# First product of the first layer by Strassen's scheme on two of three token chunks, and another order of blocks in the second layer

## The chip, the cores and the metric

The kernel runs on one core of a Trainium2 chip. The metric is device time in microseconds. Five engines work side by side: TensorE (PE) multiplies, VectorE (DVE) and ScalarE (ACT) do elementwise work and move results out of the matmul banks, GpSimd (POOL) and SyncE (SP) mostly issue DMA transfers. There are eight banks of 128 x 512 float32 into which PE accumulates.

## What is computed

Retention attention over 2 x 8 heads, 768 positions and 64 dimensions gives 1536 tokens of width 512. Two layers follow, each 512 to 2048 to 512; the weights arrive as float64.

```
state = gamma * state + k[t] (outer) v[t];  y[t] = scale * q[t] @ state
x = y as (1536, 512)
h = x @ w1_in;  g = max(h, 0) + log1p(exp(-|h|));  x = g @ w1_out
h = x @ w2_in;  g = h * clip(h + 3, 0, 6) / 6;     out = g @ w2_out
```

## The kernel before

**Number format.** Float64 weights are fetched as pairs of 32-bit words into `raw` tiles and put together into float32 (`cv` tiles) by ACT and DVE (class `Words`). Each float32 operand is split into a high and a low part, and a product is three matmuls: high by high, high by low, low by high. A weight tile `w` of 128 x 2 x 512 holds both parts.

**First layer.** Tokens come in three chunks of 512, the hidden width in 16 blocks f of 128. `gemm1` (G1) makes h for one chunk and one f: 4 slices of the contraction by 3 matmuls are 12 matmuls of 128 x 512. ACT copies h out, softplus runs on ACT and DVE (`e`, `g`, then `hi` and `lo`), and `gemm2` (G2), again 12 matmuls, adds the block into four banks (`acc`). On PE the order is G1 of unit s, then G2 of unit s - 2. All 32 weight tiles of this layer are made during chunk 0 and stay in 32 tiles of the on-chip memory for chunks 1 and 2.

**Attention.** Twelve units of 128 tokens (`attend`). Units 0 to 3 come first, 4 to 7 lie between the matmuls of chunk 0, 8 to 11 between those of chunk 1 (`spread(range(FIRST, NU), 2 * NF, 2.0)`, line 259, whose place is counted in G1 and G2). Units 8 to 11 fetch k and q also in turned blocks, by 32 small transfers each, 20 of them on SP and 12 on POOL.

**Second layer.** Tokens come in two blocks of 768, A and B. The first product is by Strassen's scheme: for a pair p of hidden blocks, seven products P1 to P7 of 6 matmuls of 128 x 384 take the place of eight. Their token operands are seven forms `xf` (sums and differences of quarters of x, made by `operands`), their weight operands four forms `wi` (made by `late_in`). A `step` is one block and one pair; its second product is 12 units of 3 matmuls of 128 x 512 into six banks (`out`), placed between the products of the next step. `STEPS` (line 243) runs A with p = 0 to 7, then B with p = 7 to 0. The forms `wi` of p < 4 go to memory and come back for B (`KEEP`), the weights of the second product come back for every step (`back`).

**What sets the order.** The list `pe` gives each task a due time; `Plan.run` then takes tasks by due time, the engines' free times, and the tiles that are free, and writes one fixed program for each engine. Every engine works through its program in order: an SP transfer that waits holds back those behind it.

Of the kernel before, what the change touches and what calls it, by code (L numbers as in the profile page):

```python
# [24 lines left out]
class Plan:  # L25


    LAG = {"PE": 0.30, "DVE": 0.12, "ACT": 0.16, "POOL": 0.16, "SP": 0.0}
    NEAR = {"PE": 0.5, "DVE": 0.15, "ACT": 0.15, "POOL": 0.3, "SP": 0.0}
# [17 lines left out]
    def __init__(self, tc):  # L47
        self.tc, self.tasks, self.pools, self.users, self.slot, self.groups = tc, [], {}, {}, {}, {}
        self.tensor, self.vector, self.scalar, self.gpsimd, self.sync = (
            self.Engine(self, getattr(tc.nc, e)) for e in ("tensor", "vector", "scalar", "gpsimd", "sync"))  # L50
# [22 lines left out]
    def run(self, log=None):  # L73
# [3 lines left out]
        left = {k: len(v) for k, v in self.users.items()}  # L77
        for _ in self.tasks:
            best = None
            for e, ts in todo.items():  # L80
                found = []
                for t in ts[:80]:
# [3 lines left out]
                    for pool in {p for p, _ in t.take}:  # L86
                        ok = self.places(pool, [k for p, k in t.take if p == pool])
                        if ok is None:
                            break
                        at = max([at] + [self.pools[pool][i] for i in ok])  # L90
# [11 lines left out]
            for pool in {p for p, _ in t.take}:  # L102
                keys = [k for p, k in t.take if p == pool]
                for key, i in zip(keys, self.places(pool, keys, at)):
                    self.pools[pool][i] = None
                    self.slot[key] = pool, i
# [27 lines left out]
def kernel(ctx, tc, q, k, v, w1_in, w1_out, w2_in, w2_out, table, out):  # L134
# [17 lines left out]
    KEEP = 4  # L152
    ONCE = 12
# [5 lines left out]
    EDGE = 9.0  # L159

    def BY_DVE(n):
        return n < 10 or n < 2 * NF and n % 4 != 0

# [13 lines left out]
    def x_of(part, c):  # L177
        key = part, c
        if key not in x_tiles:
            x_tiles[key] = (late_p if c == NC - 1 else fixed).tile([P, KD, CH], F32R, name=f"x_{part}{c}")  # L180
# [21 lines left out]
    def bank_groups(keys):  # L202
        kind, u = keys[0][0], keys[0][-1]
        if kind in ("h", "prod"):
            return [[0], [1]]
        if kind == "out":
            return [[2 + u]]
        if kind == "acc":
            return [[4, 5, 6, 7]]
# [4 lines left out]
    conv = [[("conv", m, i) for i in range(10)] for m in range(2)]  # L214
# [9 lines left out]
    room("w0", ONCE, [P, 2, CH], F32R)  # L224
    room("w", 2 * NF - LATE - ONCE, [P, 2, CH], F32R, later=[("arena", j) for j in range(LATE)])
    room("e", 2, [P, CH], F32)
    room("g", 2, [P, CH], F32)
    room("hi", 3, [P, CH], F32R)
    room("lo", 3, [P, CH], F32R)
    for name, n, shape, dtype in (("sums", 1, [P, 4, CH // 2], F32), ("xf", 7, [P, 2, 2, QT], F32R), ("tf0", 2, [P, 2, QT], F32), ("tf1", 2, [P, 2, QT], F32),  # L230
# [15 lines left out]
    cost.update(dict.fromkeys(PRODUCTS, PRODUCT))  # L246
    pe = [("Tk", 0), ("Tq", 0)]
# [11 lines left out]
    spread(range(FIRST, NU), 2 * NF, 2.0)  # L259
    n = 0  # L260
    for s in range(len(G)):
        for key in [("G1", s)] + ([("G2", s - LAG)] if s >= LAG else []):
# [3 lines left out]
    behind = [("G2", len(G) - LAG + i) for i in range(LAG)]  # L266
    for i in range(len(STEPS)):
        for name, n in PRODUCTS.items():
            pe += [(name, i)] + behind[:n]
# [23 lines left out]
    class Words:  # L293
# [47 lines left out]
        def made(self, at, fetch_at, load, give):  # L341
            T["F", self.key] = t0 = nc.add("SP", 0.45, self.fetch, due=fetch_at, take=[(f"raw{self.m}", self.raw_k)], load=load)
            t1 = nc.add("ACT", 0.65, self.bits, [t0], at - 3.5, take=[(f"cv{self.m}", self.cv_k)])
            if self.m:
# [9 lines left out]
    def weight(o, f, number):  # L354
# [3 lines left out]
        made = conv[0]  # L358
# [13 lines left out]
        part = [("w0" if number < ONCE else "w", ("w", key))]  # L372
        tail = 1.5 if BY_DVE(number) else 7.0
        t5 = x.made(use - tail, begin + 15 if number < 1 else use - tail - 8.0, 1.45 if o else 1.75, [x.raw_k])
# [7 lines left out]
        T["W", key] = [a, b]  # L382

    stash = ctx.enter_context(tc.tile_pool(name="stash", bufs=1, space=bass.MemoryType.DRAM))

    def kept(name):
        return stash.tile([P, 2 * CH], F32, name=name)

    def late_out(f):
# [4 lines left out]
        at = due["P1", f // 2] - 40.0 + 2.0 * f  # L394
        t = x.made(at, at - 10.0, 1.45, [])
# [4 lines left out]
        a = nc.add("ACT", ACS, lambda: nc.scalar.activation(part(0), x.w().bitcast(F32), AF.Copy), [t], at)  # L400
        b = nc.add("DVE", TT, lambda: nc.vector.tensor_tensor(part(1), x.w().bitcast(F32), part(0).bitcast(F32), ALU.subtract), [a], at + 0.7, give=[x.cv_k])
# [6 lines left out]
    def back(key, home, after, when):  # L408
        T["W", key] = [nc.add("SP", 0.45, lambda: nc.sync.dma_start(out=at_slot(key).rearrange("p a n -> p (a n)").bitcast(F32), in_=home),
                              [after], when, take=[("w", key)], load=1.6, hold=HOLD + when - 10.0)]  # L410

    def late_in(p):
# [3 lines left out]
        at = due["P1", p] - (20.0 if p else 12.0)  # L416
        t = [v.made(at + 2 * f, at - 10.0 + f, 1.75, [v.raw_k]) for f, v in enumerate(x)]
        sums = ("sums", ("sums", p))
        halves = slice(0, CH // 2), slice(CH // 2, CH)

        def word(f, j):
            return x[f].w().bitcast(F32)[:, halves[j]]

        def total(n):
            return at_slot(("sums", p))[:, n]
# [8 lines left out]
        s4 = nc.add("DVE", d, put(3, lambda: word(0, 1), lambda: total(1), ALU.subtract), [s2], at + 3.3)  # L434

        def pair(n):
            return at_slot(("sums", p))[:, n:n + 2].rearrange("p a n -> p (a n)")

        whole = slice(0, CH)
        for n, (source, cols, after, give) in enumerate((  # L440
                (lambda: x[0].w().bitcast(F32), whole, t, [x[0].cv_k]),
                (lambda: x[1].w().bitcast(F32)[:, halves[1]], halves[1], t, [x[1].cv_k]),
                (lambda: pair(0), whole, [s1, s2], [sums[1]]),
                (lambda: pair(2), whole, [s3, s4], [sums[1]]))):
            key = "wi", 0, p, n
# [577 lines left out]
```

## Time and profile before

| | us |
|---|---|
| median of 3 runs (576.94 to 577.71) | 577.46 |
| the profiled execution, its own time | 576.77 |
| its span, first to last instruction | 575.0 |
| PE busy | 565.5 |
| DVE busy | 386.9 |
| ACT busy | 334.9 |
| DMA traffic, MB | 91.08 |

The profile is of one execution. Busy is time in which an engine executes; matmuls overlap and their ends are modelled, so the distance between the starts of matmuls says more of PE than its busy time. A timeline row merges neighbours of one kind: start, length, engine, operation, tiles, shape, count, and in brackets the idle time before it and what ended it.

### The profile page before, as it was taken

How to read it: one execution, taken by the hardware profiler on the slowest of the kernel's cores; microseconds unless marked ns; L12 is line 12 of the kernel's file. 1: busy time of each engine (PE TensorE's matmuls, PEld its weight loads, DVE VectorE, ACT ScalarE, POOL GpSimd, SP SyncE). 2: the span in 40 equal slices, each digit the busy share in tenths (PEclk: the TensorE clock that was granted, in tenths of full speed). 3: DMA queues.
4: the chain of work that ended last, by engine and by line, in shares of the span. 5: the costliest groups of instructions: out<-in, count | busy, mean ns of one | idle time of the engine just before them, and what ended most of it. 6: DMA issues, size and time to landing. Idle time of an engine off the chain costs nothing.

```text
span 575.0 us, 9555 instructions
## 1 busy us (share of the span) xinstructions
PE 565.5 (98%) x3703; PEld 482.9 (84%) x3703; DVE 386.9 (67%) x694; ACT 334.9 (58%) x544; POOL 32.8 (6%) x61
## 2 busy tenths in 40 slices
PE   8999999999999999999999999999999999999996
PEld 7778788888788888888888988889988999888995
DVE  4999999994655446734889597997976544444342
ACT  3589889884333267945889596887644322222222
POOL 0000001044540000000000000000000000000000
PEclk9999999999999999999999999999999999999999
DMA  9998766613441206421655878486223595550003
GB/s 201 242 269 225 196 190 186 201 26 69 83 81 41 85 25 219 148 73 59 236 182 175 338 249 277 168 272 240 111 74 111 189 357 192 207 197 28 1 1 109
DMA packets 82157, 91.08 MB, mean 158 GB/s; under 512 B 48320, under 2 KB 65728, under 8 KB 82112
## 3 DMA queue, kind: packets, MB, share of 16 engines
q1 hardware_dynamic: 79856, 88.37, 48.6%
q0 software_dynamic: 2256, 2.10, 2.0%
q8 instruction: 29, 0.48, 0.3%
q14 instruction: 16, 0.13, 0.1%
HBM read 69.22 MB, written 19.92 MB: 155 GB/s over the span
## 4 chain that ended last, share of the span: by engine, by line
PE 94%; DVE 3%; ACT 2%; issue 0%; POOL 0%; ACTq 0%; DVEq 0%; POOLq 0%
PE banks L44 94%; DVE c L44 1%; ACT cv L44 1%; DVE raw L44 0%; ACT e L44 0%; ACT w L44 0%; DVE xf L44 0%; DVE cv L44 0%; ACT xf L44 0%; ACT parts L44 0%; ACT raw L44 0%; DVE parts L44 0%; DVE st L44 0%; ACT base L44 0%; DVE qT L44 0%
## 5 line engine op out<-in xcount | busy, mean ns | idle before, releaser
L44 PE MATMUL banks<-w,parts 128*128 128x512 f32 x579 | 136.9, 390 | 0.0
L44 PE MATMUL banks<-x_hi,w 128*128 128x512 f32 x384 | 127.2, 395 | 0.0
L44 PE MATMUL banks<-hi,w 128*128 128x512 f32 x384 | 126.8, 392 | 0.0
L44 PEld LDWEIGHTS banks<-w,parts 128*128 128x128 f32 x579 | 108.0, 188 | 21.3
L44 PE MATMUL banks<-xf,w 128*128 128x384 f32 x672 | 123.9, 337 | 0.5 <-ACT base L44 0.3
L44 PEld LDWEIGHTS banks<-xf,w 128*128 128x128 f32 x672 | 118.1, 188 | 4.5 <-ACT base L44 1.0
L44 PEld LDWEIGHTS banks<-x_hi,w 128*128 128x128 f32 x384 | 72.0, 188 | 15.6
L44 PEld LDWEIGHTS banks<-hi,w 128*128 128x128 f32 x384 | 72.1, 188 | 15.4
L44 PE MATMUL banks<-lo,w 128*128 128x512 f32 x192 | 74.8, 390 | 0.0
L44 PE MATMUL banks<-x_lo,w 128*128 128x512 f32 x192 | 74.4, 390 | 0.0
L44 ACT ACTIVATE g<-banks 128x512 f32<-128x512 f32 x48 | 28.4, 591 | 51.4 <-PE banks L44 51.1
L44 ACT ACTIVATE e<-c,three 128x384 f32<-128x384 f32 (+1 forms) x32 | 24.6, 768 | 55.4 <-DVE c L44 55.2
L44 ACT ACTIVATE cv<-raw,half 128x512 uint32<-128x512 uint32 x64 | 48.4, 759 | 8.9 <-DMA raw<-in_moe_w_in_dram 8.0
L44 ACT ACTIVATE cv<-raw 128x512 f16<-128x512 int32 x64 | 50.6, 790 | 0.9
L44 DVE TENSOR_SCALAR raw<-raw 128x512 f32<-128x512 f32 x96 | 40.5, 427 | 6.3 <-ACT raw L44 3.4
L44 DVE SCALAR_TENSOR_TENSOR cv<-raw,cv 128x512 uint32<-128x512 uint32 x64 | 43.8, 688 | 1.1
L44 DVE SCALAR_TENSOR_TENSOR g<-g,e 128x512 f32<-128x512 f32 x48 | 33.0, 688 | 15.1 <-ACT e L44 14.8
L44 DVE TENSOR_TENSOR c<-total,banks 128x384 f32<-128x384 f32 x16 | 8.9, 553 | 50.3 <-PE banks L44 50.2
L44 DVE TENSOR_SCALAR e<-g 128x512 uint32<-128x512 uint32 x48 | 20.4, 425 | 32.8 <-ACT g L44 32.7
L44 PEld LDWEIGHTS banks<-lo,w 128*128 128x128 f32 x192 | 36.0, 188 | 7.1
L44 PEld LDWEIGHTS banks<-x_lo,w 128*128 128x128 f32 x192 | 36.1, 188 | 7.0
L44 DVE TENSOR_TENSOR lo<-g,hi 128x512 fp32r<-128x512 f32 x48 | 33.0, 688 | 10.2 <-ACT hi L44 10.0
(85 smaller groups left out, 582.4 us busy)
## 6 DMA issues: line engine op xcount, KB each, us to landing
raw<-in_moe_w_in_dram SPq DMA_DIRECT2D x32, 512.0 KB, 4.6
raw<-in_moe_w_out_dram SPq DMA_DIRECT2D x32, 512.0 KB, 4.6
w<-stash_out SPq DMA_DIRECT2D x32, 512.0 KB, 5.2
stash_out<-raw SPq DMA_DIRECT2D x16, 512.0 KB, 3.1
stash_in<-w SPq DMA_DIRECT2D x16, 512.0 KB, 3.9
w<-stash_in SPq DMA_DIRECT2D x16, 512.0 KB, 4.2
out_dram<-ob SPq DMA_DIRECT2D x11, 256.0 KB, 2.1
q<-in_q_dram SPq DMA_DIRECT2D x8, 256.0 KB, 5.3
```

The costliest lines, as they stand in the source:

```text
L44: return self.plan.tc.keep_in_program_order(getattr(self.engine, op)(*args, **kwargs))
```

## The change

**First layer.** For f = 0 to 11 the products of chunks 1 and 2 are made together. The two chunks and the two halves of the contraction give the quarters of x, and a pair p of hidden blocks those of the weights: `early_step(p)`, p = 0 to 5, has seven products L1 to L7 of 6 matmuls of 128 x 512, six additions on DVE and two copies on ACT. `early_operands` makes seven token forms and one plain one (`xl`, 128 x 2 x 1024) once; `early_in` makes the weight forms of a pair from float32 words that chunk 0 put into memory (`words_in`). f = 12 to 15 stay plain (`PLAIN`), and come first in chunks 1 and 2.

**Consequences of it.** Both chunks must be there before the first L product, so units 8 to 11 move into chunk 0 (`spread(range(FIRST, NU), 18, 1.5)`). Chunk 2's h goes to memory (`put_by`) and comes back for its softplus; the 16 G2 of chunk 2 stand in one row after chunk 1 is done. The 32 weight tiles become 20 (`SLOTS`); w1_out's parts of f = 8 to 15 go to memory and come back in chunks 1 and 2 (`parts_out`). From the 21st weight on, ACT scales in place of DVE (`BY_ACT`).

**Second layer.** The order is A with p = 0 to 3, B with 3 to 0, B with 4 to 7, A with 7 to 4. `wi` then stays on chip between its two uses, with no way through memory. A's sums after four pairs are put aside on chip (`keep`, six tiles) and added at the end; A's seven forms `xf` go to memory and come back (`stash_x`).

```
-    STEPS = [(b, p) for b in range(2) for p in (range(NPAIR) if b == 0 else reversed(range(NPAIR)))]
+    STEPS = [(0, p) for p in range(MID)] + [(1, p) for p in (*reversed(range(MID)), *range(MID, NPAIR))] + [(0, p) for p in reversed(range(MID, NPAIR))]
+    STAGE = [0] * MID + [1] * NPAIR + [2] * (NPAIR - MID)
-    spread(range(FIRST, NU), 2 * NF, 2.0)
+    spread(range(FIRST, NU), 18, 1.5)
...
+            pe += [(name, p) for name in (("L1", "L6", "L2", "L7") if p else ("L6", "L7"))] + behind[:1] + [(name, p) for name in ("L5", "L4", "L3")] + behind[1:]
+        behind = [("G2", NF + 2 * p + i) for i in range(2)]
...
+    def put_by(f, a, at):
+        home, s = kept(f"stash_h{f}", CH), 2 * NF + f
+        c = nc.add("SP", 0.45, lambda: nc.sync.dma_start(out=home, in_=at_slot(("hs", f))), [a], at, give=[("hs", f)], load=0.8)
+        a = nc.add("SP", 0.45, lambda: nc.sync.dma_start(out=at_slot(("g", s)), in_=home), [c], due["G2", s] - LEAD + 2.0, take=[("g2", ("g", s))],
+                   load=0.8, hold=HOLD + due["G2", s] - LEAD)
...
+    def early_step(p):
...
+                for kk in range(2):
+                    for m, (l, r) in enumerate(((0, 0), (0, 1), (1, 0))):
+                        nc.tensor.matmul(bank(BANK[name]), w[:, l, kk, :], x[:, r, kk, :], start=fresh and kk == 0 and m == 0, stop=kk == 1 and m == 2, skip_group_check=not fresh)
...
+        p5 = product("P5", [])
+        d2 = add(total, mid, lambda: bank(3), [p7, d1], D["P4"] - 1.2, [total])
+        p4 = product("P4", [d2])
+        d3 = add(h[1], total, lambda: bank(4), [p5, d2], D["P3"] - 1.2, [h[1]], [total])
+        p3 = T["last product"] = product("P3", [d3])
```

**PE, in the middle of chunk 1.** Before, one pair of units: G1 (`x_hi`, `x_lo`) and G2 (`hi`, `lo`) in turn. `w_...` are weight tiles, the number is the tile's.

```order
L44 MATMUL banks<-x_hi_615,w_96 128x512
L44 MATMUL banks<-x_lo_639,w_96 128x512
L44 MATMUL banks<-x_hi_615,w_96 128x512 x2
L44 MATMUL banks<-x_lo_639,w_96 128x512
L44 MATMUL banks<-x_hi_615,w_96 128x512 x2
L44 MATMUL banks<-x_lo_639,w_96 128x512
L44 MATMUL banks<-x_hi_615,w_96 128x512 x2
L44 MATMUL banks<-x_lo_639,w_96 128x512
L44 MATMUL banks<-x_hi_615,w_96 128x512
L44 MATMUL banks<-hi_106,w_99 128x512
```

Now, at the same place, the fourth step's seven products (L1, L6, L2, L7, then L5, L4, L3) with the twelve matmuls of a G2 of chunk 1 between the two groups, of which the first and the last rows stand here.

```order
L45 MATMUL banks<-xl_1373,w_1679 128x512 x6
L45 MATMUL banks<-xl_2110,w_1685 128x512 x6
L45 MATMUL banks<-xl_1377,w_1679 128x512 x6
L45 MATMUL banks<-xl_2053,w_1786 128x512 x6
L45 MATMUL banks<-hi_95,w_78 128x512
...
L45 MATMUL banks<-hi_95,w_78 128x512
L45 MATMUL banks<-xl_2028,w_1685 128x512 x6
L45 MATMUL banks<-xl_2008,w_1758 128x512 x6
L45 MATMUL banks<-xl_2011,w_1786 128x512 x6
```

Only one G2 stands between the two groups of products; L4 alone stands between L5 and L3.

**SP, in chunk 0.** Before, the fetches of weight words follow one another after unit 7's k, q and v; `raw_...` are the five tiles into which words come.

```order
L44 DMA k_3_133<-in_k_dram 128x8x64
L44 DMA q_3_132<-in_q_dram 128x8x64
L44 DMA raw_4_73<-in_moe_w_in_dram 128x4x256
L44 DMA v_3_134<-in_v_dram 128x8x64
L44 DMA raw_0_69<-in_moe_w_out_dram 128x1024
L44 DMA raw_1_70<-in_moe_w_out_dram 128x1024
L44 DMA raw_2_71<-in_moe_w_in_dram 128x4x256
```

Now the turned blocks of unit 8 (`kb`, `qb`, 20 transfers) and a store of words stand between two fetches.

```order
L45 DMA raw_2_71<-in_moe_w_out_dram 128x1024
L45 DMA kb_0_144<-in_k_dram 32x4x32 x12
L45 DMA qb_0_145<-in_q_dram 32x4x32 x8
L45 DMA k_3_141<-in_k_dram 128x8x64
L45 DMA q_3_140<-in_q_dram 128x8x64
L45 DMA v_3_142<-in_v_dram 128x8x64
L45 DMA words_in_114<-cv_2_76 128x512
L45 DMA raw_3_72<-in_moe_w_in_dram 128x4x256
```

The blocks of units 9 and 10 stand between later fetches in the same way; before, all four came after the last fetch of the first layer's words.

## Rows read from the trace of the kernel before

**Rows 1.** The page, busy time of each engine.
```profile
PE 565.5 (98%) x3703; PEld 482.9 (84%) x3703; DVE 386.9 (67%) x694; ACT 334.9 (58%) x544; POOL 32.8 (6%) x61
```

**Rows 2.** The chain that ended last: start, length, what.
```profile
30.79 336.69 PE banks L44 x2386
```

**Rows 3.** Timeline of PE, in chunk 2 and in a step of the second layer.
```profile
302.82 0.39 PE L44 MATMUL banks<-x_hi,w 128*128 128x512 f32 x1
...
308.26 0.39 PE L44 MATMUL banks<-x_hi,w 128*128 128x512 f32 x1
...
499.73 4.37 PE L44 MATMUL banks<-xf,w 128*128 128x384 f32 x24
503.94 4.28 PE L44 MATMUL banks<-w,parts 128*128 128x512 f32 x18
508.06 1.23 PE L44 MATMUL banks<-xf,w 128*128 128x384 f32 x6
```

**Rows 4.** Groups by form: count, busy us, mean ns of one, idle before.
```profile
L44 PEld LDWEIGHTS banks<-xf,w 128*128 128x128 f32 x672 | 118.1, 188 | 4.5 <-ACT base L44 1.0 <-DVE part L44 0.5 <-DVE c L44 0.2
L44 ACT ACTIVATE cv<-raw 128x512 f16<-128x512 int32 x64 | 50.6, 790 | 0.9
L44 DVE TENSOR_SCALAR raw<-raw 128x512 f32<-128x512 f32 x96 | 40.5, 427 | 6.3 <-ACT raw L44 3.4 <-ACT cv L44 1.8
L44 DVE TENSOR_TENSOR lo<-g,hi 128x512 fp32r<-128x512 f32 x48 | 33.0, 688 | 10.2 <-ACT hi L44 10.0
L44 DVE STREAM_TRANSPOSE cv<-raw 128x512 f32<-128x512 f32 x8 | 5.7, 711 | 4.4 <-DMA raw<-in_k_dram 1.3 <-PE banks L44 1.3 <-DMA raw<-in_q_dram 1.2
L44 DVE TENSOR_TENSOR sums<-sums,cv 128x256 f32<-128x256 f32 x8 | 3.3, 418 | 0.0
```

**Rows 5.** Windows: length, busy (instructions) by engine, clock, DMA share, GB/s.
```profile
31.00:105.00 74.00, 74.00 (x761) 59.60 (x753) 71.34 (x145) 67.86 (x114) 4.03 (x4) 1.00 0.78 216
185.00:317.00 132.00, 132.00 (x685) 109.34 (x684) 85.23 (x149) 88.88 (x152) 0.00 (x0) 1.00 0.38 133
```

**Rows 6.** Timeline of PE and of DVE in chunk 0.
```profile
87.82 0.69 PE L44 MATMUL banks<-pw,vs 64*64 64x64 f32 x32
...
88.91 0.50 PE L44 MATMUL banks<-hi,w 128*128 128x512 f32 x1
...
93.90 0.68 DVE L44 TENSOR_TENSOR lo<-g,hi 128x512 fp32r<-128x512 f32 x1
...
94.58 1.15 PE L44 MATMUL banks<-qT,st 64*64 64x64 f32 x32
95.66 0.50 PE L44 MATMUL banks<-hi,w 128*128 128x512 f32 x1
95.99 0.39 PE L44 MATMUL banks<-lo,w 128*128 128x512 f32 x1
```

**Rows 7.** Timeline of SP's issues, and issues with KB and us to landing.
```profile
34.05 0.37 SPq L44 DMA_DIRECT2D raw<-in_moe_w_in_dram  x1
...
101.90 5.14 SPq L44 DMA_DIRECT2D raw<-in_moe_w_out_dram  x3
...
122.20 5.56 SPq L44 DMA_DIRECT2D raw<-in_k_dram  x12
...
143.67 3.71 SPq L44 DMA_DIRECT2D raw<-in_q_dram  x8
...
raw<-in_moe_w_in_dram SPq DMA_DIRECT2D x32, 512.0 KB, 4.6
...
w<-stash_out SPq DMA_DIRECT2D x32, 512.0 KB, 5.2
```

**Rows 8.** Timeline of PE where the second layer goes from A to B.
```profile
420.74 2.27 PE L44 MATMUL banks<-xf,w 128*128 128x384 f32 x12
423.28 2.41 PE L44 MATMUL banks<-xf,w 128*128 128x384 f32 x12 [0.27 <-ACT base L44]
425.52 4.29 PE L44 MATMUL banks<-w,parts 128*128 128x512 f32 x18
```

More of the change, by code (lines that the diff above doesn't have):

```diff
@@ L89, in run @@
                             break
+                        if pool in self.IN_ORDER:
+                            ahead = sum(len(u.take) for u in takers[pool][:takers[pool].index(t)] if u.due < self.until)
+                            if ahead + len(ok) > sum(x is not None for x in self.pools[pool]):
+                                break
                         at = max([at] + [self.pools[pool][i] for i in ok])
@@ L382, in weight, with kept @@
         T["W", key] = [a, b]
+        if not o and f // 2 in PAIRS:
+            home = homes["in", f] = kept(f"words_in{f}", CH)
+            T["S", key] = nc.add("SP", 0.45, lambda: nc.sync.dma_start(out=home, in_=x.w().bitcast(F32)), [t5], use, give=[x.cv_k] + made, load=0.8)
+        elif o and f >= KEPT:
+            home = kept(f"parts_out{f}")
+            c = nc.add("SP", 0.45, lambda: nc.sync.dma_start(out=home, in_=at_slot(("w", key)).rearrange("p a n -> p (a n)").bitcast(F32)), [a, b], use + 8.0,
+                       give=[("w", key)], load=1.6)
+            for c_of in (1, 2):
+                back(("wl", c_of, f), home, c, due["G2", c_of * NF + f] - 8.0, 2.0)
+    homes = {}
     stash = ctx.enter_context(tc.tile_pool(name="stash", bufs=1, space=bass.MemoryType.DRAM))
-    def kept(name):
-        return stash.tile([P, 2 * CH], F32, name=name)
+    def kept(name, n=2 * CH):
+        return stash.tile([P, n], F32, name=name)
     def late_out(f):
@@ L779, in gemm1 @@
-        p = nc.add("PE", GEMM, go, T["W", (m, 0, f)] + x, at, take=[("bank", ("h", s))], give=[("w", (m, 0, f))])
-        h, e, g, hi, lo = (lambda key=(n, s): at_slot(key) for n in ("h", "e", "g", "hi", "lo"))
-        r = at + GEMM
-        need = due["G2", s]
-        a = nc.add("ACT", ACP, lambda: nc.scalar.activation(g(), h(), AF.Copy), [p], r, take=[("g", ("g", s))], give=[("h", s)])
+                nc.tensor.matmul(h, w[:, a, kk, :], x_part(kk, b), start=(n == 0), stop=(n == 3 * KD - 1))
@@ new lines, in gemm1 @@
+        x = [t for name in forms_of for t in T["xl", name]] if c else [t for u in range(START) for t in ready["x", u]]
+        p = nc.add("PE", GEMM, go, T["W", (m, 0, f)] + x, at, take=[("bank", ("h", s))], give=[("w", (m, 0, f))] + [("xl", name) for name in forms_of or ()])
+        if c < 2:
+            a = nc.add("ACT", ACP, lambda: nc.scalar.activation(at_slot(("g", s)), at_slot(("h", s)), AF.Copy), [p], at + GEMM, take=[("g", ("g", s))], give=[("h", s)])
+            softplus(s, a)
+        else:
+            a = nc.add("ACT", ACP, lambda: nc.scalar.activation(at_slot(("hs", f)), at_slot(("h", s)), AF.Copy), [p], at + GEMM, take=[("hs", ("hs", f))], give=[("h", s)])
+            put_by(f, a, at + GEMM)
@@ L937, in step @@
                 f, t = (0, x + 3) if x < 3 else (1, x - 3)
-            key, w_key = ("out", b, t), ("wo", b, 2 * p + f)
-            begun, ended = i % NPAIR == 0 and q == 0, last and q == 1
+            key, w_key = ("out", stage, t), ("wo", b, 2 * p + f)
+            begun, ended = STAGE.index(stage) == i and q == 0, last and q == 1
             at = due["unit", i, n]
@@ L948, in go @@
                         nc.tensor.matmul(at_slot(key)[:, cs], l[:, y], w[:, z, cs], start=begun and m == 0, stop=ended and m == 2 and cs.stop == CH)
-            u = nc.add("PE", UNIT, go, T["parts", i, q] + T["W", w_key], at, take=[("bank", key)] if begun else [], give=[g[q], w_key])
+            u = T[key] = nc.add("PE", UNIT, go, T["parts", i, q] + T["W", w_key] + [T.get(key)], at, take=[("bank", key)] if begun else [], give=[g[q], w_key])
             if not ended:
+                continue
+            if stage == 0:
+                T["keep", t] = nc.add("ACT", ACP, lambda key=key, t=t: nc.scalar.activation(at_slot(("keep", t)), at_slot(key), AF.Copy, scale=1.0 / 6.0),
+                                      [u], at, take=[("keep", ("keep", t))], give=[key])
                 continue
```

288 lines of the change are left out of this document (207 added, 81 removed).

## The prediction

> **What bounds the kernel now.** I read the page's first part, then the chain that ended last, then PE's timeline by the starts of its matmuls, and then DVE, SP and the transfers at the places that the change touches. PE is busy for 565.5 of 575.0 us [rows 1], and the chain runs through PE alone for 336.69 us without a break, 2386 matmuls from 30.79 us on [rows 2]: the whole first layer and the beginning of the second. The starts say the same without the modelled ends: from 302.82 to 308.26 us stand one G1 and one G2, 24 matmuls of 128 x 512, at 0.2267 us each [rows 3], and I found no place in chunks 1 and 2 where the distance grows beyond a change of kind. So a matmul taken out there is worth its 0.2267 us, as long as nothing else comes last. What could is seen in two places. In chunk 0 DVE works 71.34 of 74 us [rows 5]; in chunks 1 and 2 it works only 85.23 of 132 us. In the second layer PE loses a little where block A ends and B begins [rows 8].
>
> **The sum, part by part.** It is made against the profiled execution's own time, 576.77 us (span 575.0 and 1.77 around it); the median of the runs is 577.46, 0.69 above, and I add that at the end.
>
> 1. *Matmuls.* 12 blocks in 2 chunks are 24 G1 units of 12 matmuls, 288. Six steps of 7 products of 6 are 252. 36 fewer x 0.2267 = **-8.16 us**. All other matmuls stay in kind and number. The new ones have 512 columns as the old ones, but change bank every 6. In the second layer 18 matmuls of 512 columns take 4.12 us from start to start (503.94 to 508.06), 0.2289 each [rows 3]; if the new ones go at that pace, 252 x 0.0022 = 0.55 more, if at G1's pace nothing. I take **+0.3**.
>
> 2. *The chain within an L step.* L3 adds into the bank of L5, which DVE must have read in between; only L4 covers that, 6 x 0.2267 = 1.36 us. One DVE instruction of 512 columns takes 0.688 us [rows 4], so 0.67 us are left for the handover and for whatever DVE has just begun. The nearest row is the second layer's own step: there the cover is 6 x 0.175 = 1.05 us, and the 24 matmuls still go from 499.73 to 503.94, 4.21 us, with no loss [rows 3]. DVE's work in a step: six additions x 0.688, four sums x 0.418, three low parts x 0.688 and one x 0.418 make 8.3 us; the softplus of chunk 1's two units (one word operation of 0.427, two of 0.688 each) 3.6; together 11.9 us beside 42 x 0.2267 + 2 x 2.72 = 15.0 us of PE. That fits, with the conversions of the second layer's weights in what is left. The first step has no G2 between its products and needs a token form whose tile only comes free with the last plain G1 of chunk 2. Bounds: nothing, and one DVE instruction late in each step, 6 x 0.69 = 4.1. A gain is excluded, since nothing there waits now. I take **+0.5**, nearest to the second layer's row.
>
> 3. *Chunk 0.* Units 8 to 11 move in. On DVE each has two transposes at 0.711, three operations of 512 columns at 0.688 and three of 256 at 0.418, 4.74 us; four are 19.0. Two of the new token forms fall in it as well; one of 1024 columns is an estimate, 1.23 us, going from 0.418 at 256 and 0.688 at 512 in the same step: 2.5. Out go the low parts of x of units 4 to 7 (4 x 0.688 = 2.8) and, since ACT scales the later words, 12 of the 96 word operations (12 x 0.427 = 5.1) [rows 4]. PE gets longer there too, by about 2.8 us a unit: two of its three parts take 1.09 us (87.82 to 88.91) and 1.08 (94.58 to 95.66) [rows 6], the third about half of that; four are 11.2. So DVE's balance against PE is 19.0 + 2.5 - 2.8 - 5.1 - 11.2 = 2.4 us worse over a stretch of some 110 us. The margin now: the low part of the ninth G2 is ready at 94.58 us and first used at 95.99, 1.41 us later [rows 6]. Bounds: 0 (a gain is excluded, since PE has no gap there to lose), and 4 us if in addition a fetch of words comes late (the slower rival, below). I take **+0.4**, near the lower end, since the 2.4 us are spread over the stretch and the margin there covers most of them.
>
> 4. *Transfers.* Chunk 2's h goes to memory and back: two legs, each no longer than the 5.2 us of a load twice the size [rows 7], 10.4 us, against the 24 us of lead in the code: hidden, and 10 us at once if it weren't. w1_out's parts come back 16 times, asked for some 10 us ahead and landing in 5.2: hidden while the queue is short. It is longest at the end of chunk 2, where the seven `xf` (768 KB each, 5.4 MB) are stored between these loads: at the 216 GB/s of the first window in rows 5 they need 25 us, and the code begins to make the forms 30 us ahead of their use. Bounds 0 and 3; I take **+0.2**.
>
> 5. *Second layer.* The change from A to B costs today 4.78 us for 24 matmuls of `xf` (420.74 to 425.52 [rows 8]) instead of 4.21, 0.57 us. It moves to the fifth step and stays. A second change, B to A, is new: its operands come by transfers, and ask nothing of DVE and ACT. Each of the seven loads of 768 KB has 14.5 us from the last use of its tile to the next (six products of 6 x 0.175 and 36 unit matmuls x 0.229), against 5.2 us for a load of 512 KB [rows 7]. What is left is the emptying of six banks, as at the change that there is. Bounds: -0.5, if the moved change finds DVE and ACT freer than today's, and 1.0; I take **+0.3**, half of today's change. The order itself removes no PE work: its gain (16 stores and 16 loads of `wi` fewer) lies beside PE, where nothing waits for it.
>
> Sum: -8.16 + 0.3 + 0.5 + 0.4 + 0.2 + 0.3 = -6.46; 576.77 - 6.46 = 570.3, and with 0.69 for the median **571.0 us**.
>
> *A rule against it.* PE's weight loads take 188 ns each, and for the 384-column products 672 of them fill 118.1 us, 0.176 each [rows 4], which is the whole distance from start to start there (4.21 / 24 = 0.175 [rows 3]): at 384 columns the load sets the pace. At 512 columns 0.2267 is well above it. The Trainium skill, Perfetto Trace Analysis, section Identifying the Most-Contended Engine, says that matmul busy time is no measure of how near the limit PE is, and that the busy share of the loads is one. That share is 482.9 of 575.0, 84% [rows 1]; if the loads set the pace everywhere, the 36 pairs would be worth 36 x 0.188 = 6.8 us in place of 8.16, and the sum would give 572.4. For the 512-column matmuls the rows say otherwise.
>
> **The rivals.**
> - *The L steps wait for DVE (574.6).* Part 2 at its upper bound, 4.1 in place of 0.5. For it: DVE works its list in order, and softplus and weight forms stand between the additions. Against it: 3 us of 15 are free, and the second layer does the same with less cover. It is the nearest to being decided by chance, step by step.
> - *Slower: chunk 0 starves for words (579.5).* A unit's 20 small transfers hold SP for 5.56 us (12) and 3.71 (8), 9.3 together [rows 7]. Before, they stood behind all fetches of the first layer's words; now three such blocks stand between fetches. DVE uses a word tile every 3.0 us (24 fetches from 34.05 to 107.0 [rows 7]), and five are in hand, 15.2 us. A fetch that is held back needs 9.3 + 4.6 to landing [rows 7] + two ACT passes of about 0.79 [rows 4], 15.5 us. That is just even. If the fetches in hand are one fewer when the block begins, each block costs DVE 3.3 us; three of them, less the 1.4 us of margin, give 8.5 on PE, and 571.0 + 8.5 = 579.5. It decides from four words in hand. Against it: DVE has other work while it waits, the moved units' own.
> - *The loads set PE's pace (572.4)*, as worked out above.
> - *Nothing waits (569.3)*: parts 2 to 5 at their lower bounds, 577.46 - 8.16.
>
> The Trainium skill, Perfetto Trace Analysis, section What "DMA-bound" means, names as one kind of transfer bound that the issuing engine's track is solid with issues. The two SP rows above are such a stretch, of 9.3 us; the trace of before doesn't show PE waiting for it, since the fetches were over by then.
>
> **How the numbers follow.** Chances: the forecast with all that lies between 568.5 and 573, the loads' rival and the one without waits among it, 0.74; the L steps' rival, up to 576.3, 0.14; chunk 0's, above 576.3, 0.12, of which 0.08 is slower than 578.6. The range takes the first two, whose lower end is the lower bounds with half a microsecond for the other small terms (0.69 of offset, changes of kind), 568.5, and whose upper end is the L rival with parts 3 to 5 also half way up, 576.0. A difference of 0.2%, 1.15 us, is about what a measurement of this kernel can tell from none: faster than 576.3 0.88, within it 0.04, slower 0.08.
>
> **What would show it.** Right: 348 matmuls that read `xl` at 0.227 to 0.229 us from start to start; PE's idle time within the L steps below 1 us in all; the ninth to sixteenth G2 of chunk 0 without a gap before their first low-part matmul; two changes of block with some 0.5 to 1 us lost at each. Wrong, and where: a gap before each L3 (in steps of 0.69 us), PE waiting in chunk 0 with DVE idle and SP's row of small issues solid, a G2 of chunk 2 that waits for a load of w1_out, or a first product of the last stage that waits for `xf`. The forecast falls if any one of the parts 2 to 5 passes 4 us.

## The result: 4.4 us slower

The changed kernel takes 581.76 us (median of 6 runs, 580.12 to 583.77), the kernel before 577.41 (6 runs, 576.86 to 578.65). The ratio is 1.0072, 95% interval 1.0048 to 1.0095: slower by 0.7%, where 571.0 us were forecast. The profiled execution of the changed kernel took 581.40 us (span 579.6).

PE has as much less work as forecast, and waits instead. The page's busy line, against [rows 1], and the windows of the changed kernel (length, then busy time of PE, PEld, DVE, ACT, POOL, the clock, DMA share, GB/s):

```profile
PE 561.5 (97%) x3667; PEld 476.6 (82%) x3667; DVE 430.4 (74%) x768; ACT 358.0 (62%) x578; POOL 33.7 (6%) x61
```
```profile
31.00:96.00 65.00, 64.47 (x711) 51.78 (x713) 61.87 (x123) 58.16 (x96) 16.97 (x27) 1.00 0.87 245
96.00:152.00 56.00, 49.07 (x592) 37.94 (x589) 43.21 (x79) 43.19 (x71) 15.69 (x26) 1.00 0.78 211
152.00:253.00 101.00, 101.00 (x516) 83.29 (x515) 78.65 (x138) 59.68 (x99) 0.00 (x0) 1.00 0.46 160
253.00:313.00 60.00, 59.63 (x263) 48.73 (x261) 56.90 (x103) 46.08 (x80) 0.00 (x0) 1.00 0.92 335
```

Between 96 and 152 us, where chunk 0 ends and units 9 to 11 run, PE stands still for 6.93 us while DVE works 43.21 and ACT 43.19 of 56 us: nobody is full, all wait. From 152 to 253 us, in the Strassen steps, PE has no gap. The same stretch of the kernel before has PE at 56.00 of 56.

To see where the rest went I use one landmark, the first product of the third step of the second layer. Timeline of PE before, and after:

```profile
342.27 4.40 PE L44 MATMUL banks<-xf,w 128*128 128x384 f32 x24
```
```profile
344.98 4.35 PE L45 MATMUL banks<-xf,w 128*128 128x384 f32 x24
```

Up to there the changed kernel should be 8.16 us ahead and is 2.71 behind, 10.9 us lost; from there to the end it takes 579.6 - 344.98 = 234.6 us against 232.7, 1.9 lost. Of the first, 1.0 lies before the first G1 (27.81 against 26.80 us, rows below), 6.9 are the gaps of 96 to 152 us, and a gap costs about 0.15 more than its idle time, since the matmul ahead of it ends by a model (0.39 us in the rows, against 0.2267 from start to start): eight gaps, 1.2 by this estimate. Two later gaps (0.37 at 267.58, 0.55 at 329.01) are half of the remaining 1.7; the other half I could not place.

```profile
26.80 2.09 PE L44 MATMUL banks<-x_hi,w 128*128 128x512 f32 x8
```
```profile
27.81 2.08 PE L45 MATMUL banks<-x_hi,w 128*128 128x512 f32 x8
```

What the gaps wait for, in the timelines of PE, DVE and SP of the changed kernel (start, length, what; idle time before and its releaser in brackets):

```profile
129.17 0.50 PE L45 MATMUL banks<-x_hi,w 128*128 128x512 f32 x1 [1.33 <-ACT g L45]
...
136.96 0.73 PE L45 MATMUL banks<-x_hi,w 128*128 128x512 f32 x2 [0.75 <-DMA w<-cv]
...
146.01 0.50 PE L45 MATMUL banks<-lo,w 128*128 128x512 f32 x1 [0.93 <-DVE lo L45]
...
150.50 0.69 PE L45 MATMUL banks<-qT,kT 64*64 64x64 f32 x32 [1.71 <-DVE qT L45]
```
```profile
144.67 0.71 DVE L45 STREAM_TRANSPOSE kT<-kb 128x512 f32<-128x512 f32 x1 [3.05 <-DMA qb<-in_q_dram]
...
148.91 0.71 DVE L45 STREAM_TRANSPOSE qT<-qb 128x512 f32<-128x512 f32 x1 [0.96 <-PE banks L45]
```
```profile
109.98 8.85 SPq L45 DMA_DIRECT2D kb<-in_k_dram  x12
118.92 0.50 SPq L45 DMA_DIRECT2D raw<-in_moe_w_in_dram  x1
119.54 0.51 SPq L45 DMA_DIRECT2D raw<-in_moe_w_out_dram  x1
120.14 4.76 SPq L45 DMA_DIRECT2D qb<-in_q_dram  x8
...
134.15 8.98 SPq L45 DMA_DIRECT2D kb<-in_k_dram  x12
143.24 4.09 SPq L45 DMA_DIRECT2D qb<-in_q_dram  x8
```

The 20 small issues of units 10 and 11 hold SP for 13.6 and 13.1 us here, against 5.56 + 3.71 = 9.3 in [rows 7]. The releasers on PE differ from gap to gap, but behind the large ones stands a transfer that came late: at 144.67 and 148.91 DVE turns blocks of unit 11 that have only just landed (the trace has the landing of the last piece of k at 144.54, of q at 148.79 us; the releasers in brackets are inferred, and name others there). The chain that ended last between 96 and 152 us says the same. These are the transfers in it, 23.5 of the 56 us, about half of it words and half of it blocks:

```profile
101.45 7.38 DMA raw<-in_moe_w_out_dram
...
119.54 5.03 DMA raw<-in_moe_w_out_dram
124.59 2.69 DMA qb<-in_q_dram
...
134.15 6.50 DMA kb<-in_k_dram
...
146.90 1.89 DMA qb<-in_q_dram
```

SP's own waits for landings from 55 to 152 us (total, times, longest):

```profile
SPq L45 <- DMA raw<-in_moe_w_out_dram: 6.9, 5, 1.9
SPq L45 <- DMA raw<-in_moe_w_in_dram: 3.1, 3, 1.5
SPq L45 <- DMA kb<-in_k_dram: 1.3, 3, 0.7
```

With smaller ones they are 13.0 us; in the kernel before there are none in that stretch. The program says why an issue waits for a landing: SP's transfers signal on eight semaphores in turn, and each issue first waits for its semaphore, that is for the transfer eight places ahead. From the listing of SP in the changed kernel:

```
48 L45 DMA raw_2_71<-in_moe_w_out_dram 128x1024 [waits DMAHW0_49,DVE_49,Activation_49]
49 L45 DMA kb_0_144<-in_k_dram 32x4x32 [waits DMAHW1_49]
50 L45 DMA kb_0_144<-in_k_dram 32x4x32 [waits DMAHW2_49]
...
55 L45 DMA kb_0_144<-in_k_dram 32x4x32 [waits DMAHW7_49]
56 L45 DMA kb_0_144<-in_k_dram 32x4x32 [waits DMAHW0_49]
```

So the eighth small issue behind a fetch of words stands until those 512 KB have landed (row 56 waits for row 48), and everything behind it stands too. The Trainium skill, DMA: Bandwidth & Descriptors, section Why a DMA increments its semaphore by 16 and not by 1, asks for one semaphore for each slot in flight. This program has eight such slots on SP, and the waits above are what they cost it.

### The profile page after: what moved, and what is told of

It reads as the page before. It is cut to its first block, busy times and chain, and to the rows that moved or that the text cites. A ratio compares the mean times of both kernels' runs of the same rounds, so it can differ in the third digit from the quotient of the medians.

```text
span 579.6 us, 9697 instructions
## 1 busy us (share of the span) xinstructions
PE 561.5 (97%) x3667; PEld 476.6 (82%) x3667; DVE 430.4 (74%) x768; ACT 358.0 (62%) x578; POOL 33.7 (6%) x61
## 4 chain that ended last, share of the span: by engine, by line
PE 75%; DMA 9%; ACT 7%; DVE 5%; issue 1%; SPq 1%; DVEq 0%; POOL 0%; ACTq 0%; POOLq 0%
PE banks L45 75%; DMA raw<-in_moe_w_out_dram 4%; ACT cv L45 2%; DMA stash_out<-raw 1%; DMA kb<-in_k_dram 1%; ACT raw L45 1%; ACT w L45 1%; SPq L45 1%; DMA stash_h<-hs 1%; DMA g<-stash_h 1%; DVE raw L45 1%; DMA qb<-in_q_dram 1%; DVE cv L45 1%; ACT e L45 1%; ACT parts L45 1%
## 5 line engine op out<-in xcount | busy, mean ns | idle before, releaser
L45 PE MATMUL banks<-xf,w 128*128 128x384 f32 x672 | 125.4, 338 | 2.4 <-ACT base L45 1.5
L45 PE MATMUL banks<-hi,w 128*128 128x512 f32 x384 | 125.2, 393 | 0.0
L45 PE MATMUL banks<-xl,w 128*128 128x512 f32 x348 | 82.5, 391 | 0.4 <-DVE hs L45 0.4
L45 PEld LDWEIGHTS banks<-xl,w 128*128 128x128 f32 x348 | 64.9, 188 | 14.7 <-DVE hs L45 0.8
L45 DVE TENSOR_SCALAR raw<-raw 128x512 f32<-128x512 f32 x84 | 35.7, 426 | 15.6 <-ACT raw L45 13.2
L45 PE MATMUL banks<-x_hi,w 128*128 128x512 f32 x128 | 42.9, 401 | 2.1 <-ACT g L45 1.3
L45 ACT ACTIVATE hi<-g 128x512 fp32r<-128x512 f32 x48 | 30.0, 627 | 21.1 <-DVE g L45 12.4
L45 DVE TENSOR_TENSOR parts<-c,parts 128x768 fp32r<-128x768 f32 x32 | 30.6, 957 | 14.2 <-ACT parts L45 13.9
L45 ACT ACTIVATE e<-e 128x512 f32<-128x512 f32 x48 | 29.6, 627 | 18.2 <-DVE e L45 18.0
L45 ACT ACTIVATE parts<-c 128x768 fp32r<-128x768 f32 x32 | 27.0, 844 | 17.3 <-DVE c L45 17.2
```

Source lines behind the costliest of these rows:

```text
L45: return self.plan.tc.keep_in_program_order(getattr(self.engine, op)(*args, **kwargs))
```

## Experiments

Medians with the number of runs; "before" stands at 576.96 to 577.41 us beside them. "Third step" is the landmark above, from the profile. The theory: small transfers cost the time in chunk 0. The rivals: too much work on DVE and ACT there; the traffic of the new stores; the second layer's order.

### What costs the time in chunk 0

**e1_blocks_once.**
```diff
-            ikb, iqb = (task("SP", ..., blocks(n), ...) for n in ("kb", "qb"))
+            if u == FIRST:
+                ready["blocks"] = [task("SP", ..., blocks(n), ...) for n in ("kb", "qb")]
+            ikb, iqb = ready["blocks"]
...
```


> The changed kernel, but only unit 8's k and q are fetched in 32-row blocks; the transposes of units 9 to 11 read unit 8's blocks again, so 96 of the 128 transfers of 16 KB are left out and the scores of units 9 to 11 are not the reference's. The work of PE, DVE and ACT is the same. Theory (small transfers): PE's idle time between 96 and 152 us, 6.9 us in the changed kernel, comes from SP's blocks of 20 small issues, which hold back the words behind them and land late themselves; without them it falls below 2 us and the time to 575 to 577. Rival (DVE and ACT have too much to do in chunk 0): same work, so 580 to 582. Rival (the new stores of words and parts fill the DMA engines): 579 to 582.

Measured 572.84 (4 runs): 8.9 us back, more than expected. Window of 96 to 152 us:
```profile
96.00:152.00 56.00, 55.27 (x686) 43.77 (x681) 49.28 (x92) 48.90 (x83) 1.72 (x2) 1.00 0.83 261
```
DVE and ACT have the same work in chunk 0; in this window they are now busy for 49 of 56 us, and PE loses 0.73. The work of DVE and ACT is not the cause.

**e2b_parts_once.**
```diff
+            home, c = homes.get("parts", (None, None))
+            if home is None:
+                home, c = ... one store, as before; homes["parts"] = home, c
```


> The changed kernel with one of the eight stores of w1_out's parts; the loads that bring them back read that one, so seven stores of 512 KB (3.5 MB, most of them between 100 and 160 us) are left out and the second products of chunks 1 and 2 use wrong weights for half of the blocks. Theory (small transfers): these stores are one of many things in SP's queue, 1 to 2 us of the loss: 579.5 to 581. Rival (traffic of the new stores slows every landing in chunk 0): the 6.9 us mostly vanish, 575 to 577.

581.68 (4 runs): nothing. PE is busy for 49.22 of the 56 us, as in the changed kernel. These stores are not the cause; the 12 stores of words were not taken away alone.

**e5_split** (20 issues as five pieces of 4).
```diff
-            ikb, iqb = (task("SP", ..., blocks(n), ...) for n in ("kb", "qb"))
+            for x, (n, to) in enumerate((("kb", ikb), ("qb", iqb))):
+                for p in range(SHARE[n] + 1):
+                    to.append(task("SP", 0.48 * 4, blocks(n, ps), ..., d["S"] - 25.0 + x + 2.0 * p, ...))
```


> The changed kernel with each unit's 20 small issues on SP put in as five pieces of 4, between which word fetches can stand; no transfer is left out. If it is the length of the block that holds back the words (a fetch behind it waits 9 us and more), a fetch now waits for 2 to 4 us and most of the 6.9 us comes back: 575.5 to 578. If it is the number of small transfers and their own lateness (unit 11's q block lands at 148.8 us, just before it is used), little changes: 580 to 583.

583.35 (4 runs): nothing comes back. But the run does not test the length of a block as it was meant to, since only unit 8's pieces let words through. In SP's timeline the pieces of unit 9 stand from 84.3 to 100.7 us with one k and one v between them, those of unit 11 from 134.6 to 148.6, and those of unit 10 follow one another as before:
```profile
114.14 3.04 SPq L45 DMA_DIRECT2D kb<-in_k_dram  x4
117.28 1.84 SPq L45 DMA_DIRECT2D qb<-in_q_dram  x4
119.17 2.25 SPq L45 DMA_DIRECT2D kb<-in_k_dram  x4
121.46 1.85 SPq L45 DMA_DIRECT2D qb<-in_q_dram  x4
123.36 1.86 SPq L45 DMA_DIRECT2D kb<-in_k_dram  x4
```
Whether shorter blocks would help stays open.

**e4_two_tiles** and **e7_later.**
```diff
-              {"kb": 1, "qb": 1, "k": 2, ...
+              {"kb": 2, "qb": 2, "k": 2, ...
```
```diff
-    spread(range(FIRST, NU), 18, 1.5)
+    spread(range(FIRST, NU), 22, 1.5)
```


> The changed kernel with two tiles instead of one for the blocks of k and of q, so that a unit's blocks can be asked for before those of the unit ahead are turned. All transfers stay. If the blocks are late because the next unit's must wait for the tile (24 us of POOL's waiting is for it): 576 to 579. If issue time and landing time of the small transfers are what is short, asking earlier only moves the wait to the words: 580 to 584.

> The changed kernel with the twelve pieces of units 8 to 11 each four places (G1 or G2, some 11 us) later in PE's order, so that the blocks of units 10 and 11 are fetched when most words have landed. All work and all transfers stay. Theory (small transfers and words of the first layer compete): 576 to 580. If the blocks' own way is too long whenever they come: 581 to 584.

584.61 and 586.30 (4 runs each), both above all that was expected. Neither asking earlier nor running later brings anything back, and both lose more: in e7 PE stops once for 3.39 us behind a late v, and then runs at half the clock (last section).

**e3_blocks_pool** (`SHARE = {"kb": -1, "qb": -1}`).

> The changed kernel with all 128 small transfers of units 8 to 11 issued by POOL instead of 80 by SP and 48 by POOL. The same transfers of 16 KB go through the DMA engines, but SP's queue holds only words, stores and plain loads. If SP's issuing time is what was short (80 issues of 0.43 us and more between the words), most of the 8.9 us that came back without them comes back here too: 573 to 577. If the small transfers themselves are what is short (the DMA engines, or blocks that land just before their use), nothing is gained, and POOL's 32 issues of 0.55 us for a unit, 17.6 us, make them later still: 581 to 586.

598.34 (4 runs), far beyond the upper end. POOL's 32 issues for a unit also hold up its weight transfers: PE waits once for 8.86 us for `w<-cv` at 96.70 us. It does not speak on SP's queue.

**e8_quarter_bytes** and **e9_quarter_issues**, the pair that tells issues from packets.
```diff
-                        for p in range(NP):
-                            (...).dma_start(out=tile_of(n)[r, p]..., in_=src[g, e, :, p])
+                        for p in range(NP):
+                            (...).dma_start(out=tile_of(n)[r, p]...[:, :1], in_=src[g, e, :, p, :1])
```
```diff
-    SHARE = {"kb": 2, "qb": 1}
+    SHARE = {"kb": 0, "qb": 0}
...
-                        for p in range(NP):
-                            (...).dma_start(out=tile_of(n)[r, p]..., in_=src[g, e, :, p])
+                        near = {"qb": q, "kb": k}[n][b, g, :16 * 32, e * 32:(e + 1) * 32].rearrange("(y t) d -> t y d", t=32)
+                        nc.sync.dma_start(out=tile_of(n)[r].rearrange("t p (x d) -> t (p x) d", x=4), in_=near)
```


> The changed kernel with all 128 small issues of units 8 to 11, but each fetches a quarter (32 rows of one packet of 128 B in place of four); the rest of the tiles stays zero, so the scores of units 8 to 11 are not the reference's. Queue positions, tiles and waits stay as they are. If the cost of the small transfers is their number in the queue: 580 to 583. If it is their packets in the DMA engines, most of the 8.9 us comes back: 573 to 576.

> The changed kernel with 32 transfers of 64 KB in place of the 128 of 16 KB, all issued by SP; each reads rows of one head that lie evenly, so bytes and packets of 128 B are as many as in the changed kernel, and the scores of units 8 to 11 are not the reference's. If the cost is the number of issues: 573 to 576, as without the transfers. If it is the packets: 580 to 583.

e8 577.86 (10 runs), e9 574.94 (4 runs). Windows of e8 and of e9, and SP's waits for landings in e8:
```profile
96.00:152.00 56.00, 50.56 (x583) 39.02 (x584) 45.62 (x82) 44.89 (x74) 14.32 (x26) 1.00 0.71 203
```
```profile
96.00:152.00 56.00, 56.00 (x683) 44.50 (x683) 47.27 (x84) 46.40 (x77) 1.76 (x2) 1.00 0.95 268
```
```profile
SPq L45 <- DMA raw<-in_moe_w_out_dram: 5.8, 5, 1.6
...
SPq L45 <- DMA raw<-in_moe_w_in_dram: 3.1, 4, 1.1
```
With a quarter of the packets PE still stands for 5.4 us and SP still waits 10 us for landings; with a quarter of the issues the DMA engines are busier (0.95 against 0.78), SP waits for no landing, and PE has no gap at all. So it is the number of small issues and not their bytes. In which queue, e9 alone does not tell: SP's 80 became 32, and POOL's 48 went too (its busy time falls from 15.69 to 1.76 us). c6, below, has 64 on POOL, none on SP, and no gap. e8 does gain 3.9 us, more than "nothing" and less than "most": packets have a part too, of 1.5 us in the gaps of this window; 0.84 us of e8's gain are an earlier first G1 (26.97 us). The Trainium skill, Perfetto Trace Analysis, section What "DMA-bound" means, says that large descriptors matter where the issuing engine is the bound; here the packets stayed at 128 B and fewer issues did it. How much of it is the issue's own time (0.43 us), how much the wait for the eighth ahead, and how much the length of a block, no run separates.

### Ways around it, and the second layer

**e6_pe_turned** and **f1_k_on_pe.** `todo` has "T" for units 8 to 11 as well, and k and q (in f1 only k) are loaded whole and turned on PE. In these runs, and in all below that turn blocks on PE, the pieces of units 8 to 11 stand 1.2 places apart in place of 1.5.
```diff
-        if ph:
-            kt = task("DVE", TT, in_blocks("kb", "kT"), [ikb], ...)
+        tp = task("PE", cost["Tk"], turned("k"), [ik, ...], ...)
+        kt = task("ACT", ACP, ... tile_of("kT"), bank(("kP", u)) ...)
```


> The changed kernel with units 8 to 11 turned on PE as units 4 to 7 are: no small transfer is left, one q load of 256 KB for each unit instead. PE gets 32 more transposes of 128 x 128; 64 of them take 9.76 us in the profile of the kernel before, so 4.9 us. DVE loses two block transposes of 0.71 us for each unit, ACT gets one copy of about 0.6. Theory (small transfers cost 8.9): 581.8 - 8.9 + 4.9 = 577.8, between 576.5 and 579. If the move of the units as such was the cost (ACT and DVE full): 585 to 587.

> The changed kernel with k of units 8 to 11 turned on PE, q still fetched in blocks: 64 of the 128 small transfers are gone (48 of SP's 80), PE has 16 more transposes, 2.4 us. If each small transfer costs alike (8.9 us for 96, so 5.9 for 64): 581.8 - 5.9 + 2.4 = 578.3. If it is a queue that overflows, the first half removed brings nearly all of the 8.9: 575.3 to 576.5.

e6 579.56 (7 runs), just above the expected range; f1 579.87 (8 runs, 577.57 to 584.16, a wide spread), nearer to the sum in which each small transfer costs alike than to a queue that overflows. In e6 PE has 56.00 of 56 us in the window, and the third step begins at 341.12, 4.35 after e1's 336.77: near the 4.9 for the transposes. But from there to the end it takes 237.6 us, 3.0 more than the changed kernel: the second layer loses most of what the first gained.

**o1_order_alone**, **s1_strassen_alone**, **s3_all_pe_old_order**: the two halves of the change, apart.
```diff
-    STEPS = [(b, p) for b in range(2) for p in (range(NPAIR) if b == 0 else reversed(range(NPAIR)))]
+    STEPS = [(0, p) for p in range(MID)] + [(1, p) ...] + [(0, p) ...]
```


> The kernel before with the new order of the second layer alone (A0-3, B3-0, B4-7, A7-4, the token forms stored and fetched back, the later halves of the weights converted later); the first layer stays as it was, but for two tiles instead of three for the high part of h. In the changed kernel the second layer from its second step to the end takes 250.6 us against 248.5. Theory (the order itself costs that, by conversions that fall into the steps): 579 to 580. Rival (the second layer of the changed kernel is late because its first layer ran late and left work over): 577 to 578. My recorded sum has 0.3 for it: 577.7.

> The changed kernel with the second layer in the old order (A0-7, B7-0) and its old stores, so Strassen's scheme and the move of units 8 to 11 alone. The new order alone cost 580.1 against 577.1, 3.0 us. If the two halves of the change add up: 581.8 - 3.0 = 578.8, between 578 and 580. If the second layer's loss in the changed kernel is another (work that the late first layer leaves over): 581 to 582, since that work is left over here too.

> Strassen's scheme with units 8 to 11 wholly turned on PE (no small transfer) and the second layer in the old order. If the costs add up: 579.6 - 3.0 = 576.6, between 575.8 and 577.6, so about the time of the kernel before. In its profile PE has no idle time from 96 to 152 us and the second layer takes 248 to 249 us from its second step. If the second layer's loss comes from what the first leaves over: 579 to 580.

o1 580.10 (5 runs), s1 582.38 (4 runs), s3 578.66 (7 runs). On the old first layer the new order costs 3.0 us, with the later conversions of w2 that belong to it and two tiles in place of three for `hi`; but taking it back in the changed kernel gains nothing (582.4 against 581.8), and 0.9 in e6's. The halves don't add up. From the third step to the end: before 232.7, o1 233.9, s1 235.5, s3 235.5. So Strassen's first layer makes even the old second layer slower by 2.7. A reason that offers itself is DVE at the end of the first layer, where the softplus of chunk 2 is done in one piece. From 253 to 313 us it works 56.90 of 60 us in the changed kernel (above); in the kernel before, and then in e8 and e9:

```profile
253.00:313.00 60.00, 60.00 (x266) 49.70 (x265) 44.27 (x77) 44.60 (x77) 0.00 (x0) 1.00 0.38 136
```
```profile
253.00:313.00 60.00, 60.00 (x265) 49.22 (x265) 56.17 (x101) 45.27 (x79) 0.00 (x0) 1.00 0.93 341
```
```profile
253.00:313.00 60.00, 60.00 (x270) 50.06 (x269) 52.17 (x91) 42.21 (x75) 0.00 (x0) 1.00 0.90 331
```

But e8, with DVE fuller, takes 233.9 us from the third step to the end, and e9 236.2, both with the new order and the late conversions. So how full DVE is there does not tell what the second layer takes, and the cause of the 2.7 us stays open. Of o1's 3.0 us its profiled execution, the lowest of its five times, shows 1.7; the rest I could not place.

**c3_all_pe_w2_earlier** and **c4_two_units_on_pe.**
```diff
-        at = due["P1", USED[f // 2]] - (40 - 2.0 * f if f < 2 * MID else 20)
-        t = x.made(..., hold=(HOLD + at - 24) * (f >= 2 * MID))
+        at = due["P1", USED[f // 2]] - (40 - 2.0 * f if f < 2 * MID else 40)
+        t = x.made(..., hold=(HOLD + at - 60) * (f >= 2 * MID))
```


> Units 8 to 11 turned on PE (579.6 with the new order), and the later eight blocks of w2_out fetched and converted from 36 us earlier on, in the steps between 350 and 400 us, where no conversion falls. In that kernel's profile the second layer takes 253.5 us from its second step, with waits of 1.15 (base) and 1.45 (c) at 424 and 473 us behind conversions. If late conversions are the cause: 576 to 577.5, and these two waits are gone. If the second layer's loss is of another kind: 579 to 580.

> Units 8 and 9 by blocks as in the changed kernel, units 10 and 11 turned on PE (16 more transposes, 2.4 us), and the earlier conversions of w2_out. Waits in chunk 0 come late in it, with units 9 to 11; if the small transfers of units 10 and 11 cause most of them: first layer as fast as with all on PE or 2 faster, 574 to 577. If those of units 8 and 9 alone fill the queue already: 578 to 581.

c3 577.02 (10 runs), 2.5 less than e6 for an edit that moves conversions only; in its profile, the slowest of the ten runs, the gaps at 424 and 473 us are gone (others of 1.31 and 0.69 stand at 346 and 379). c4 577.08 (10 runs): one half of the PE work, but in its profile, again the slowest run, 3.6 us of waits in the window are back. How a conversion holds up PE, in ACT's and PE's timeline of the changed kernel:

```profile
422.60 0.76 ACT L45 ACTIVATE cv<-raw,half 128x512 uint32<-128x512 uint32 x1 [1.33 <-DMA raw<-in_moe_w_out_dram]
...
427.60 0.46 ACT L45 ACTIVATE base<-banks 128x384 f32<-128x384 f32 x1
```
```profile
428.12 2.35 PE L45 MATMUL banks<-xf,w 128*128 128x384 f32 x12 [1.07 <-ACT base L45]
```
ACT works in order: it stands 1.33 us for a word that was asked for late, and `base`, which P2 needs, stands behind it.

**c6b_q_on_pe_k_by_pool**, **c6_k_on_pe_q_by_pool**, **c8_k_on_pe_old_order**: no small issue on SP.
```diff
-    SHARE = {"kb": 2, "qb": 1}
+    SHARE = {"kb": 2, "qb": -1}
```
This is c6, on top of f1 and of c3's edit; c6b has q on PE and `{"kb": -1, "qb": 1}`; c8 is c6 with the old `STEPS` and without c3's edit.

> The changed kernel with q of units 8 to 11 turned on PE (16 more transposes, 2.4 us), the 64 small transfers of k all issued by POOL, and the later half of w2_out converted earlier. SP issues no small transfer. Theory (SP's issues wait for the landing of the one eight places ahead, so 20 small issues hold up the words): no idle time of PE from 96 to 152 us, first layer as with a quarter of the issues plus 2.4 us, second layer 249 to 251 us from its second step: 574 to 576. If small issues cost the same from any queue: 578 to 580.

> The same with k turned on PE and q's 64 small transfers issued by POOL. ACT has one copy of 0.6 us more for each unit than with q on PE; otherwise the same sum: 574 to 576.5 if SP's queue is the cause, 578 to 580 if small issues cost the same from any queue.

> The version with k turned on PE and q's blocks issued by POOL (575.0), but with the second layer in the old order, whose conversions of w2 stand where they stood in the kernel before. From the third step to the end the new order with earlier conversions takes 233.7 us, the old order behind Strassen's first layer 235.5 in two profiles. If a late first layer's left-over work is the cause of that: 576 to 577.5, since DVE is as full as before at the end of the first layer. If the old order costs nothing once chunk 0 has no waits (232.7, as in the kernel before): 573.5 to 574.5.

c6 **574.97 us** (4 runs; ratio to before 0.9959, interval 0.9946 to 0.9971): faster than both kernels. Its window:
```profile
96.00:152.00 56.00, 56.00 (x665) 44.38 (x664) 46.09 (x85) 45.31 (x78) 25.39 (x43) 1.00 0.79 243
```
Its third step begins 2.75 us after e9's, against 2.4 for the 16 transposes, and SP waits for no landing from 55 to 152 us. The first products of the third step in e9 and in c6:
```profile
336.49 2.27 PE L45 MATMUL banks<-xf,w 128*128 128x384 f32 x12
```
```profile
339.24 2.27 PE L45 MATMUL banks<-xf,w 128*128 128x384 f32 x12
```
c6b came to 579.04 (12 runs): in its profile POOL's sixteen issues for unit 9 end at 103.1 us, the last block lands 6.4 us after its issue, and PE stands for 3.50 us at 110.25. That is the time of the rival: here small issues cost from POOL's queue too. In c6 the blocks are q's, which the plan turns 0.7 us later than k's; that this is the difference between the two, no run shows. c8, with the old order, came to 577.09 (10 runs): its third step begins at 339.17, as in c6, but the rest takes 235.9 us against 233.7. With a first layer that does not wait, the new order with earlier conversions is worth 2.1 us.

## Why the prediction was wrong, step by step

1. *Matmuls* (-8.16, +0.3 for pace): right. In the changed kernel 24 products of the Strassen steps go from 211.04 to 216.48 us, 0.2267 each, so the 0.3 were not needed:
```profile
211.04 5.60 PE L45 MATMUL banks<-xl,w 128*128 128x512 f32 x24
216.48 0.39 PE L45 MATMUL banks<-hi,w 128*128 128x512 f32 x1
```
2. *The chain within an L step* (+0.5): right, and it cost less. PE waits for 0.37 us from 152 to 313 us in all. The rival of the L steps (574.6) did not happen, nor did that of the weight loads.
3. *Chunk 0* (+0.4, bounds 0 to 4): this step failed. It measured 6.9 us of idle time and some 1.2 around it. The balance of DVE's work was the wrong thing to weigh: e1 has that work, and 0.73 us of idle time. The bound of 4 added one late fetch of words to that balance; the small transfers' own issues were a term only in a rival. With a quarter of these issues, at the same bytes, the idle time is gone (e9).
4. *Transfers* (+0.2): right as far as it went. h's detour shows as one gap of 0.37 us, and taking away seven of the eight stores of w1_out's parts brought nothing (e2b).
5. *Second layer* (+0.3, bounds -0.5 to 1.0): mis-sized, 1.9 us. The changes of block were weighed. But of PE's gaps from the third step on, 1.7 us in all against 0.3 in the kernel before, 1.07 are the one at 428.12 us behind a conversion of w2's words, which the step did not mention. What moving these conversions is worth, c3 shows on e6's first layer (2.5 us). In the changed kernel no run moved them alone, c8 changes them and the order together, and the 2.7 us that the old order loses behind Strassen's first layer (s1, s3) are not explained.

With chunk 0 free of gaps, e9 reaches the third step at 336.49 us, and its first G1 at 27.85 is 1.05 later than before; without that, 335.44. Parts 1 to 4 of the sum put it at 342.27 - 6.76 = 335.51. So what failed on the way there is in part 3 and in that start. That the two agree to 0.1 us is partly luck: the 0.8 us that parts 1 and 2 allowed for pace and chain were not needed there, and small gaps elsewhere took their place.

The rival *Slower: chunk 0 starves for words* (579.5, 0.08) named the place and the thing, SP's small transfers, and came nearest. It was priced by a block of 9.3 us taken from a stretch where SP had nothing else to do; among words and stores the same issues took 13 to 16 us (16.1 for unit 9, 12.19 + 3.91). Its mechanism, words held behind a block, is half of what the chain of 96 to 152 us shows; the other half is the blocks' own landing, which the rival did not count. e5, meant to separate the two, does not. Its point of decision (four words in hand) covers the first half alone. What could have told was there to see: twenty issues a unit, and a program in which each waits for the eighth ahead.

## What to carry to other kernels

Count a queue's issues as work, 20 small ones as 20, and look in the program for what each waits for: with a fixed number of transfers in flight, as with the eight semaphores here, a small one behind large ones takes their landing time. A duration of an issue from a quiet stretch is a lower bound in a busy one. When work is moved, look also at what it leaves to later: here the second layer lost 1.9 us where the sum had 0.3, and how busy an engine was in the stage ahead did not tell it.

## What was not expected of the hardware

After a gap PE can pay twice. In e7 PE stood 3.39 us, and the granted clock was at 0.50, the lower level of 1.2 GHz, in the 2 us that followed, and at 0.64 in the next 2 (timeline of PE and windows of e7):

```profile
116.89 1.08 PE L45 MATMUL banks<-pt,vs 64*64 64x64 f32 x32 [3.39 <-DVE vs L45]
```
```profile
117.00:119.00 2.00, 2.00 (x65) 1.88 (x66) 1.97 (x5) 1.20 (x3) 0.00 (x0) 0.50 1.04 387
119.00:121.00 2.00, 2.00 (x6) 1.58 (x7) 1.97 (x4) 1.97 (x5) 0.00 (x0) 0.64 1.07 416
```

The gaps of the changed kernel's profile, 1.71 us at most, left the clock at 1.00. In f1 it fell behind a shorter gap than e7's, and stood at the lower level two microseconds later (timeline of PE and window of f1):

```profile
129.01 0.63 PE L45 MATMUL banks<-ident,k 128*128 128x128 f32 x4 [1.91 <-DMA k<-in_k_dram]
```
```profile
131.00:133.00 2.00, 2.00 (x7) 1.52 (x6) 1.91 (x4) 2.00 (x3) 0.00 (x0) 0.50 0.43 124
```

The 1.0 us before the first G1 is not shown to be of that kind. The first eight transposes behind the warm-up take 0.21 us each instead of 0.11 to 0.15, but the granted clock reads 1.00 there in both profiles. Other kernels with that same beginning reach the first G1 between 26.97 and 28.80 us, and o1, whose beginning is the kernel before's, at 27.54 against 26.80, so it goes with the execution and not with the change; its cause stays open.
